# Another slot plan in an attention kernel: the 64-query tile third, V products in five slots, normalisation a slot later

## The chip, the cores and the metric

One core of a Trainium2 chip. The metric is the device time of one execution in microseconds (us). The whole computation is one program and one launch.

## The reference, cut to what matters

```python
def _attn_ref(q, k, v, w1, b1, w2):                      # q, k, v: (4, 8, 576, 64)
    scores = np.matmul(q, k.transpose(0, 1, 3, 2)) / np.sqrt(64)
    psi_rel = np.log1p(np.abs(pos[:, None] - pos[None, :]))
    psi_i = np.log1p(np.maximum(pos[:, None], 1.0))
    h = np.maximum((psi_rel / psi_i)[..., None] @ w1 + b1, 0.0)
    scores = scores + (h @ w2).transpose(2, 0, 1)[None]  # one bias table per head
    attn = np.exp(scores - np.max(scores, axis=-1, keepdims=True))
    attn = attn / (np.sum(attn, axis=-1, keepdims=True) + 1e-09)
    return np.matmul(attn, v)
x = attn_out.transpose(0, 2, 1, 3).reshape(2304, 512)
h = x @ w_in                                              # 512 -> 2048
out = (h * np.cos(h)) @ w_out                             # 2048 -> 512
```

## The kernel before

The program has three stages. The engines are named as in the profile: PE (TensorE), DVE (VectorE), ACT (ScalarE), POOL (GpSimd), SP (SyncE, which here only issues DMAs). Each engine runs its own instructions strictly in the order in which the program issues them.

**Bias (0 to about 61 us).** 36 groups of 16 query positions are computed and written to DRAM (`sc`), and read back as bias tiles by query tile: tile 4 (the last 64 queries) is computed first and loaded early (L348), tiles 0 to 3 are loaded in steps 19, 27, 35 and 36 of the loop (L346). The loop also turns the first keys and queries (`T_FIRST`, L335).

**Attention (about 61 to 346 us).** A *unit* is a pair of heads of one batch: 16 units (L71). A unit has five *slots* (L528), one for each tile of queries: tiles 0 to 3 have 128 queries for each of the two heads; tile 4 has the 64 last queries of both heads in one tile of 128 rows. `tiles` (L331) is the order of the tiles in the slots. `slot(i)` (L542) issues for every engine what belongs to slot `i` of 80 and works on several tiles at once:

- the tile of this slot (`now`): scores by `qk` (L380), in 12 matmuls (6 for tile 4), since queries and keys are split in a high and a low part (high x high, high x low of the keys, low of the queries x high, for each half of the columns and each head). DVE adds the bias and takes the minimum (L402; the scores are negated);
- the tile of the slot before (`last`): exponential and row sum on ACT (`softmax_exp`, L418); then the sum plus 1e-9 and its reciprocal on DVE (`recip`, L431), and the normalisation of the exponentials on POOL (`norm`, L439);
- the tile of three slots before (`prev`): transposes on PE (`ptrans`, L453; `ptrans_left`, L463), copied out of PSUM half by ACT and half by DVE (`keep_main`, L476; `keep_left`, L487);
- the product with V of an earlier unit (`pv`, L503), in five chunks of keys for each half of the queries; the fifth has the last 64 keys. `PV_EARLY` (L537) gives the chunks to slots: half 0 in slots 0 and 1, half 1 in slots 3 and 4, none in slot 2. ACT copies the result (`keep_x`, L523);
- the next units' queries and keys: the load (`LOAD_PLAN`, L538), the turn on PE (`T_EARLY`, L536; "x" is the last 64 positions of keys and queries), ACT's copy (`keep_turned`, L189), and the split in high and low parts on POOL (`split`, L163; `POOL_PLAN`, L529): step 0 gives the high part, steps 1 and 2 the low part of columns 0 to 319 and 320 to 639. Keys were turned two units ahead, queries one;
- one eighth of the first feed-forward weights in ten slots (`W_PLAN`, L539): these come as 64-bit floats and are converted by integer passes: `abs_w` on ACT (L89), steps 0, 0.5, 1 and 2 of `widen_w` on DVE (L99 to L105), step 3 on ACT (L107), step 4 on POOL (L109).

Scores have a ring of two PSUM buffers (`ps_s`, L365), one for each head. So a slot's product for head 0 can start when DVE has reduced head 0 of the slot before. Tile 4 uses one buffer; the other (`spare`, L414) takes the turned keys in that slot. Exponentials have four buffers (`pp`, L366).

**Feed-forward (about 346 us to the end).** 96 steps of two products on PE, with the cosine between them on ACT and DVE. Its first two steps (L774 to L779) are issued between the last slots of the attention; in unit 15 POOL already splits the feed-forward's input (`split_x`, L493), four parts in slots 0 to 3.

Of the kernel before, what the change touches and what calls it, by code (L numbers as in the profile page):

```python
# [23 lines left out]
def f(ap):  # L24
    return ap.bitcast(F32)
# [3 lines left out]
def kernel(  # L29
# [42 lines left out]
    NU = len(units)  # L72
# [16 lines left out]
    def abs_w(fc, part):  # L89
        b = wk.tile([128, 512], F32, tag="wb", name="wb")  # L90
        nc.scalar.activation(out=b, in_=f(raw[fc, part][:, :, 1]), func=AF.Abs)
        wabs[fc, part] = b
# [18 lines left out]
    with tc.manual_schedule():  # L111
# [27 lines left out]
        def load(u, x):  # L139
            hp, b = units[u]  # L140
            src = {"q": q, "k": k, "v": v}[x]
            pair_ = src[b, 2 * hp : 2 * hp + 2]
            if x == "v":
                t = vN[u % 2]
                for h in range(2):
                    nc.sync.dma_start(
                        out=t[:, 4 * h : 4 * h + 4, :], in_=pair_[h, 0:512].rearrange("(c p) d -> p c d", p=128)
                    )
                for h in range(2):
                    nc.sync.dma_start(out=t[64 * h : 64 * h + 64, 8, :], in_=pair_[h, 512:576])  # L150
                return
            m = 5 if x == "k" else 4
            t = (lk if x == "k" else ld).tile([128, m, 2, D], F32, tag=x, name=f"n{x}")
            for h in range(2):
                nc.sync.dma_start(out=t[:, 0:4, h], in_=pair_[h, 0:512].rearrange("(p r) d -> p r d", r=4))  # L155
            if x == "k":
                for i, o in ((k, 0), (q, 64)):
                    nc.sync.dma_start(
                        out=t[o : o + 64, 4], in_=i[b, 2 * hp : 2 * hp + 2, 512:576].rearrange("h p d -> p h d")
                    )  # L160
            nat[u, x] = t

        def split(u, x, step=None):  # L163
            n = turned[x]
            if x == "k":
                if u not in kN:
                    kN[u] = tp.tile([128, 2, 640], F32R, tag="kN", name="kN")
                o = kN[u]
            else:
                o = qTs[u % 2]  # L170
            if step in (None, 0):
                nc.gpsimd.tensor_scalar(o[:, 0], n, 1.0, 1.0, ALU.mult, ALU.mult)
            for i in range(2):
                c = slice(320 * i, 320 * i + 320)
                if step in (None, 1 + i):
                    nc.gpsimd.tensor_tensor(o[:, 1, c], n[:, c], f(o[:, 0, c]), ALU.subtract)
# [78 lines left out]
        wparts = [(fc, p) for fc in range(WPRE) for p in range(2)]  # L255
# [72 lines left out]
            )  # L328
            nc.sync.dma_start(out=sc[t][gi, :, 0 : RB - 1], in_=rt[:, 0 : RB - 1])

        tiles = [0, 1, 2, 3, 4]  # L331
        for i in range(WPRE):
            W[i] = wpre[i]
        ACT_H = [k for k in range(36) if k % 4 != 3]
        T_FIRST = {11: (0, "k"), 12: (0, "x"), 13: (0, "q"), 15: (1, "k")}  # L335
        S_FIRST = {13: "k", 14: "q"}
        todo = [(t, gi) for t in (4, 0, 1, 2, 3) for gi in range(len(groups[t]))]
        held, hts = None, bias_hid(0)
        for n in range(len(todo) + 1):
            now = hts  # L340
            if n < len(todo):
                hts = bias_hid(n + 1) if n + 1 < len(todo) else None
                ps = bias_rows(n, now)
            if held:
                bias_store(*held)
            if n in (19, 27, 35, 36):  # L346
                load_bias(0, (19, 27, 35, 36).index(n))
            if n == 11:  # L348
                load_bias(0, 4)
            held = (n, ps)  # L350
            if n == 6:
                for x in "kq":
                    load(1, x)
            if n in T_FIRST:
                keep_turned(T_FIRST[n][1], turn(*T_FIRST[n], bank()))
            if n in S_FIRST:
                split(0, S_FIRST[n])
            if n == 20:
                load(2, "k")
        stage.close()  # L360

        ps_t = opened(tail, "ps_t", 1, "left", PSUM)
# [68 lines left out]
        def recip(u, j, step):  # L431
            n = 2 if tiles[j] < 4 else 1
            if step == 0:
                nc.vector.tensor_scalar(dn[u, j][:, 0:n], dn[u, j][:, 0:n], 1e-9, None, ALU.add)
            else:
                rc[u, j] = sv.tile([128, 2], F32, tag="rc", name="rc")
                nc.vector.reciprocal(rc[u, j][:, 0:n], dn[u, j][:, 0:n])  # L437

        def norm(u, j, h):  # L439
            p, r = P[u, j], rc[u, j][:, h : h + 1]  # L440
            if tiles[j] == 4:
                nc.gpsimd.tensor_scalar(p[:, 576:640], p[:, 512:576], r, 1.0, ALU.mult, ALU.mult)
            p = p[:, 576 * h : 576 * h + 576]
            nc.gpsimd.tensor_scalar(p, p, r, 1.0, ALU.mult, ALU.mult)  # L444

        def heads_of(x):
            return range(2 if tiles[x[1]] < 4 else 1)
# [75 lines left out]
        def keep_x(u, hf):  # L523
# [4 lines left out]
        jobs = [(u, j) for u in range(NU) for j in range(5)]  # L528
        POOL_PLAN = [  # L529
            ([], []),  # L530
            ([("k", 0)], [("k", 1)]),
            ([], [("k", 2)]),
            ([("q", 0)], [("q", 1)]),
            ([("q", 2)], []),
        ]
        T_EARLY = [(1, "x"), None, (1, "q"), None, (2, "k")]  # L536
        PV_EARLY = [[(-1, 0, (0, 1))], [(-1, 0, (2, 3, 4))], [], [(-1, 1, (0, 1))], [(-1, 1, (2, 3, 4))]]  # L537
        LOAD_PLAN = [[(2, "q")], [(3, "k")], [], [], [(1, "v")]]  # L538
        W_PLAN = [("abs", 2), (0, 3), (0.5, 4), (1, 5), (2, 6), ("load", 6), (3, 7), (4, 7)]  # L539
        get = lambda i: jobs[i] if 0 <= i < len(jobs) else None  # L540

        def slot(i):  # L542
            u, j = divmod(i, 5)
            now, last, prev = get(i), get(i - 1), get(i - 3)
            if now:
                spare = qk(u, j)
            if last:
                for h in heads_of(last):
                    softmax_exp(*last, h)
            if prev:  # L550
                if prev[1] in (0, 2):
                    alloc_half(prev[0], prev[1] // 2)
                pm = ptrans(*prev)
            left = prev and tiles[prev[1]] < 4
            tu, tx = T_EARLY[j] or (0, None)
            tx = tx if now and u + tu < NU else None
            t = bank() if left or tx in ("x", "q") else None
            if left:
                pl = t[:, 0:128]
                ptrans_left(*prev, pl)  # L560
            if tx:
                pt = turn(u + tu, tx, {"x": t and t[:, 128:256], "q": t, "k": spare}[tx])
            for du, hf, chunks in PV_EARLY[j]:
                if 0 <= u + du < NU:
                    pv(u + du, hf, chunks)
            if prev:
                keep_main(*prev, 0, pm[0])
            if tx:
                keep_turned(tx, pt)
            for du, hf, chunks in PV_EARLY[j]:  # L570
                if 0 <= u + du < NU and 4 in chunks:
                    keep_x(u + du, hf)
            if last:
                recip(*last, 0)
                recip(*last, 1)
            if prev:
                keep_main(*prev, 1, pm[1])
            if left:
                keep_left(*prev, pl)
            for x, step in POOL_PLAN[j][0]:  # L580
                if u + 1 < NU:
                    split(u + 1, x, step)
            if last:
                for h in heads_of(last):
                    norm(*last, h)
            for x, step in POOL_PLAN[j][1]:
                if u + 1 < NU:
                    split(u + 1, x, step)
            if now:
                for du, x in LOAD_PLAN[j]:  # L590
                    if u + du < NU:
                        load(u + du, x)
                hp, b = units[u]
                if b == B - 1 and hp + 1 < HP:
                    load_bias(hp + 1, tiles[j])
                if u == NU - 1 and j < KD:
                    split_x(0, 0, j)
                for step, at in W_PLAN:
                    w, r = divmod(i - 0 - at, 10)
                    if r == 0 and 0 <= w < len(wparts):  # L600
                        if step == "load":
                            if w + 2 < len(wparts):
                                load_w(*wparts[w + 2])
                        elif step == "abs":
                            abs_w(*wparts[w])
                        else:
                            widen_w(*wparts[w], step)
# [226 lines left out]
```

## Time and profile before

| | |
|---|---|
| median of 3 runs | 756.83 us (754.45 to 757.5) |
| profiled execution | 754.29 us, its span 752.5 us |
| PE busy in the span | 716.7 us (95%) |
| DVE, ACT, POOL busy | 596.7, 442.2, 404.0 us |
| mean granted clock of PE | 0.981 |
| stretch 0 to 61 us (bias) | PE busy 50.59, DVE 49.16, ACT 46.07, POOL 5.87 us |
| stretch 61 to 345.63 us (attention) | PE busy 265.76, DVE 222.44, ACT 203.72, POOL 213.28 of 284.63 us |
| stretch 345.63 to 752.5 us (feed-forward) | PE busy 400.38, DVE 325.07, ACT 192.46, POOL 184.84 of 406.87 us |

The span is the time from the first to the last instruction of one execution. An engine is busy while an instruction of it runs. Ends of matmuls are modelled: successive ones overlap in the records by up to a tenth of a microsecond, so lengths from one start to the next are the better ones. "PEclk" is the share of TensorE's full clock that was granted: 1.00 is 2.4 GHz, 0.50 is 1.2 GHz. "[0.46 <-DVE m L402]" behind an instruction means that its engine stood idle 0.46 us before it, until the instruction of line 402 on DVE that writes `m` was done.

### The profile page before, as it was taken

The numbers are of one execution on the slowest core, as the hardware profiler recorded it, in microseconds if no ns is written. First come the engines' busy times: TensorE is split into PE (matmuls) and PEld (weight loads), VectorE is DVE, ScalarE is ACT, GpSimd is POOL, SyncE is SP. The second block draws the span as 40 slices with busy tenths as digits, with TensorE's granted clock in tenths as the row PEclk, the third lists the DMA queues.
The fourth block names the chain that finished last, engine by engine and source line by source line (L and its number), as shares of the span: only waits on it lengthen the run. The fifth ranks groups of instructions, "written<-read, shape, count | busy, mean of one in ns | idle before, by whom it ended". The sixth has DMA issues, their size and how long they took to land.

```text
span 752.5 us, 15721 instructions
## 1 busy us (share of the span) xinstructions
PE 716.7 (95%) x5786; PEld 574.4 (76%) x5786; DVE 596.7 (79%) x1307; ACT 442.2 (59%) x948; POOL 404.0 (54%) x486
## 2 busy tenths in 40 slices
PE   6987899999999999988999999999999999999997
PEld 3764666666666666657998989898888989899995
DVE  8964878788787878964779788899898998976655
ACT  6966577777787777753555555444545454533332
POOL 0203687777878777784256546364463554564300
PEclk9988799999999999999999999999999999999999
DMA  7776425432652551100010101010101011001112
GB/s 223 243 253 198 96 49 148 126 96 61 184 120 49 128 154 33 46 29 1 28 57 29 57 28 57 29 57 28 57 29 57 28 43 42 1 29 57 43 42 85
DMA packets 83917, 58.64 MB, mean 78 GB/s; under 512 B 61824, under 2 KB 70144, under 8 KB 83840
## 3 DMA queue, kind: packets, MB, share of 16 engines
q1 hardware_dynamic: 83840, 57.63, 27.2%
q8 instruction: 46, 0.75, 0.4%
q14 instruction: 31, 0.25, 0.1%
HBM read 42.00 MB, written 15.61 MB: 77 GB/s over the span
## 4 chain that ended last, share of the span: by engine, by line
PE 83%; DVE 10%; issue 3%; DMA 2%; ACT 1%; SPq 1%; POOL 0%; DVEq 0%; POOLq 0%; ACTq 0%
PE ph L636 26%; PE po L691 25%; PE pv L513 10%; PE s L389 9%; DVE P L402 5%; PE pm L451 5%; PE pa L307 4%; PE pt L464 2%; DMA sc<-rt 1%; PE spare L186 1%; DVE PT L474 1%; DVE ht L291 1%; DVE gl L665 1%; DMA nk<-in_k_dram 1%; SPq L155 1%
## 5 line engine op out<-in xcount | busy, mean ns | idle before, releaser
L402 DVE CUSTOM_DVE_ANT_0 P<-s,bt 128x576 f32<-128x576 f32 x144 | 103.9, 753 | 52.1 <-PE s L389 31.6
L444 POOL TENSOR_SCALAR P<-P,rc 128x576 f32<-128x576 f32 x144 | 112.5, 794 | 39.4 <-DVE rc L437 31.8
L640 ACT ACTIVATE a<-ph,quarter 128x384 int32<-128x384 f32 x96 | 55.8, 581 | 107.9 <-PE ph L636 106.7
L646 DVE SCALAR_TENSOR_TENSOR r<-a,ph 128x384 f32<-128x384 int32 x96 | 52.9, 551 | 77.7 <-ACT a L640 77.6
L422 ACT ACTIVATE P<-P,m 128x576 f32<-128x576 f32 x144 | 110.3, 770 | 5.7 <-DVE m L402 5.4
L498 POOL TENSOR_TENSOR xs<-xT,xs 128x384 fp32r<-128x384 f32 x96 | 107.0, 1114 | 8.0
L636 PE MATMUL ph<-xs,wpre 128*128 128x384 f32 x576 | 109.5, 338 | 0.9 <-DVE a L655 0.9
L389 PEld LDWEIGHTS s<-kN,qT 64*128 64x128 f32 (+1 forms) x864 | 71.9, 190 | 49.8 <-DVE m L402 24.6
L389 PE MATMUL s<-kN,qT 64*128 64x288 f32 (+1 forms) x864 | 95.4, 317 | 14.4 <-DVE m L402 13.5
L636 PE MATMUL ph<-xs,w 128*128 128x384 f32 x576 | 108.3, 337 | 0.5 <-DVE a L655 0.5
L636 PEld LDWEIGHTS ph<-xs,wpre 128*128 128x128 f32 x576 | 101.8, 188 | 7.1 <-DVE a L655 2.1
L636 PEld LDWEIGHTS ph<-xs,w 128*128 128x128 f32 x576 | 101.3, 188 | 5.6 <-DVE a L655 1.6
L651 ACT ACTIVATE r<-r,hpi 128x384 f32<-128x384 f32 x96 | 59.3, 618 | 69.7 <-DVE r L647 69.7
L497 POOL TENSOR_SCALAR xs<-xT 128x384 fp32r<-128x384 f32 x96 | 62.1, 646 | 45.9 <-PE ph L636 45.9
L513 PE MATMUL pv<-PT,vN 128*64 128x320 f32 (+1 forms) x512 | 77.3, 424 | 2.3 <-ACT PT L471 2.3
L691 PE MATMUL po<-w,gh 128*128 128x512 f32 x288 | 75.3, 396 | 0.0
L691 PE MATMUL po<-wpre,gh 128*128 128x512 f32 x288 | 75.2, 396 | 0.0
L665 DVE TENSOR_TENSOR gl<-a,gh 128x384 fp32r<-128x384 f32 x96 | 74.1, 772 | 0.6 <-ACT gh L659 0.6
L109 POOL TENSOR_TENSOR w<-wb,w 128x512 fp32r<-128x512 f32 x16 | 20.8, 1299 | 90.2 <-ACT w L107 90.2
L647 DVE SCALAR_TENSOR_TENSOR r<-a,r 128x384 f32<-128x384 int32 x96 | 61.8, 644 | 3.3
L659 ACT ACTIVATE gh<-a 128x384 fp32r<-128x384 f32 x96 | 49.9, 520 | 23.1 <-DVE a L655 22.3
L691 PEld LDWEIGHTS po<-w,gh 128*128 128x128 f32 x288 | 53.5, 188 | 8.9 <-ACT gh L659 0.2
(83 smaller groups left out, 1207.4 us busy)
## 6 DMA issues: line engine op xcount, KB each, us to landing
sc<-rt SPq DMA_DIRECT2D x36, 295.5 KB
raw<-in_moe_w_in_dram SPq DMA_DIRECT2D x16, 512.0 KB
raw<-in_moe_w_out_dram SPq DMA_DIRECT2D x16, 512.0 KB
bt<-sc SPq DMA_DIRECT2D x16, 288.0 KB
nk<-in_k_dram SPq DMA_DIRECT2D x32, 128.0 KB
nq<-in_q_dram SPq DMA_DIRECT2D x32, 128.0 KB
vN<-in_v_dram SPq DMA_DIRECT2D x32, 128.0 KB
bt<-sc SPq DMA_DIRECT2D x16, 256.0 KB
```

Source lines behind the costliest of these rows:

```text
L389: nc.tensor.matmul(s[h][:, hf, 0:HALF], qTs[u % 2][r, a, 128 * t : 128 * t + 128] if t < 4 else qTs[u % 2][:, a, 512:640], kN[u][r, b, o : ...
L402: nc.vector.tensor_tensor_reduce(neg.rearrange("p (a x) -> p a x", a=2), s[h][:, :, 0:HALF], bias[hp, t, h].rearrange("p (a x) -> p a x", ...
L422: nc.scalar.activation(out=P[u, j][:, 576 * h : 576 * h + 576], in_=neg, func=AF.Exp, bias=m[:, 0:1], scale=-1.0, accum_out=dn[u, j][:, h ...
L444: nc.gpsimd.tensor_scalar(p, p, r, 1.0, ALU.mult, ALU.mult)
L497: nc.gpsimd.tensor_scalar(h, src, 1.0, 1.0, ALU.mult, ALU.mult)
L498: nc.gpsimd.tensor_tensor(l, src, f(h), ALU.subtract)
L513: nc.tensor.matmul(ps[64 * h : 64 * h + 64, 0 : WQ[hf]], a, m, start=(c == 0), stop=(c == 4), tile_position=(r.start, 64 * h), skip_group_ ...
L636: nc.tensor.matmul(ps, a, x, start=(i == 0), stop=(i == 3 * KD - 1))
L647: nc.vector.scalar_tensor_tensor(r, n, -TWO_PI_LO, r, ALU.mult, ALU.add)
L651: nc.scalar.activation(out=r, in_=r, func=AF.Sin, scale=SIN_SCALE, bias=hpi)
L665: nc.vector.tensor_tensor(gl, a, f(G[key][0]), ALU.subtract)
L691: nc.tensor.matmul(O[n][i], a[:, 128 * i : 128 * i + 128], w, start=(i0 == 0 and p == 0), stop=(i0 == GF - 1 and p == 2),)
```

## The change

The order of the tiles becomes 0, 1, 4, 2, 3, so the 64-query tile is third and the spare score buffer falls into slot 2. Keys are turned one unit ahead, in slot 2, queries in slot 0 and the last 64 positions in slot 1; one turn of keys in the bias stage is dropped. POOL's splits move: queries to slots 2 and 3, keys to slots 3 and 4. V chunks go to all five slots. The loads of queries and keys move by one and two slots. The weight passes on DVE move to slots 0 and 2 (of an even and an odd unit), the two last steps to slot 3 of the odd unit, and the first `abs_w` to the end of the bias stage. The sum and reciprocal (`recip`) are now those of the tile of two slots before (`late`) and come first in the slot, ahead of the reductions on DVE; the normalisation follows on POOL in that slot, ahead of all splits.

```diff
@@ -328,11 +328,11 @@
             )
             nc.sync.dma_start(out=sc[t][gi, :, 0 : RB - 1], in_=rt[:, 0 : RB - 1])
 
-        tiles = [0, 1, 2, 3, 4]
+        tiles = [0, 1, 4, 2, 3]
         for i in range(WPRE):
             W[i] = wpre[i]
         ACT_H = [k for k in range(36) if k % 4 != 3]
-        T_FIRST = {11: (0, "k"), 12: (0, "x"), 13: (0, "q"), 15: (1, "k")}
+        T_FIRST = {11: (0, "k"), 12: (0, "x"), 13: (0, "q")}
         S_FIRST = {13: "k", 14: "q"}
         todo = [(t, gi) for t in (4, 0, 1, 2, 3) for gi in range(len(groups[t]))]
         held, hts = None, bias_hid(0)
@@ -357,6 +357,8 @@
                 split(0, S_FIRST[n])
             if n == 20:
                 load(2, "k")
+            if n == len(todo):
+                abs_w(*wparts[0])
         stage.close()
 
         ps_t = opened(tail, "ps_t", 1, "left", PSUM)
@@ -528,20 +530,23 @@
         jobs = [(u, j) for u in range(NU) for j in range(5)]
         POOL_PLAN = [
             ([], []),
-            ([("k", 0)], [("k", 1)]),
-            ([], [("k", 2)]),
+            ([], []),
             ([("q", 0)], [("q", 1)]),
-            ([("q", 2)], []),
+            ([("q", 2), ("k", 0)], []),
+            ([("k", 1), ("k", 2)], []),
         ]
-        T_EARLY = [(1, "x"), None, (1, "q"), None, (2, "k")]
-        PV_EARLY = [[(-1, 0, (0, 1))], [(-1, 0, (2, 3, 4))], [], [(-1, 1, (0, 1))], [(-1, 1, (2, 3, 4))]]
-        LOAD_PLAN = [[(2, "q")], [(3, "k")], [], [], [(1, "v")]]
-        W_PLAN = [("abs", 2), (0, 3), (0.5, 4), (1, 5), (2, 6), ("load", 6), (3, 7), (4, 7)]
+        T_EARLY = [(1, "q"), (1, "x"), (1, "k"), None, None]
+        PV_EARLY = [[(-1, 0, (0, 1))], [(-1, 0, (2, 3))], [(-1, 0, (4,))], [(-1, 1, (0, 1, 2))], [(-1, 1, (3, 4))]]
+        LOAD_PLAN = [[], [(2, "q")], [], [(3, "k")], [(1, "v")]]
+        W_PLAN = [("abs", -1), (0, 0), (0.5, 2), (1, 5), (2, 7), ("load", 7), (3, 8), (4, 8)]
         get = lambda i: jobs[i] if 0 <= i < len(jobs) else None
 
         def slot(i):
             u, j = divmod(i, 5)
-            now, last, prev = get(i), get(i - 1), get(i - 3)
+            now, last, late, prev = get(i), get(i - 1), get(i - 2), get(i - 3)
+            if late:
+                recip(*late, 0)
+                recip(*late, 1)
             if now:
                 spare = qk(u, j)
             if last:
@@ -570,20 +575,14 @@
             for du, hf, chunks in PV_EARLY[j]:
                 if 0 <= u + du < NU and 4 in chunks:
                     keep_x(u + du, hf)
-            if last:
-                recip(*last, 0)
-                recip(*last, 1)
             if prev:
                 keep_main(*prev, 1, pm[1])
             if left:
                 keep_left(*prev, pl)
-            for x, step in POOL_PLAN[j][0]:
-                if u + 1 < NU:
-                    split(u + 1, x, step)
-            if last:
-                for h in heads_of(last):
-                    norm(*last, h)
-            for x, step in POOL_PLAN[j][1]:
+            if late:
+                for h in heads_of(late):
+                    norm(*late, h)
+            for x, step in POOL_PLAN[j][0] + POOL_PLAN[j][1]:
                 if u + 1 < NU:
                     split(u + 1, x, step)
             if now:
```

## Rows read from the trace of the kernel before

**Rows 1.** Stretches: busy time of each engine, then granted clock, DMA share, GB/s.

```profile
core 0: us, PE busy (x) PEld busy (x) DVE busy (x) ACT busy (x) POOL busy (x), PEclk, DMA share, GB/s
61.00:80.49 19.49, 12.71 (x97) 9.66 (x97) 9.79 (x30) 10.14 (x25) 8.79 (x12) 0.68 0.64 154
99.08:312.27 213.19, 205.96 (x2352) 140.36 (x2350) 175.80 (x520) 162.95 (x428) 166.83 (x216) 1.00 0.41 101
312.27:345.63 33.36, 29.06 (x282) 18.95 (x281) 21.57 (x59) 17.81 (x41) 23.73 (x31) 0.95 0.14 42
324.00:327.00 3.00, 3.00 (x12) 1.21 (x11) 1.78 (x8) 2.11 (x5) 2.92 (x4) 0.50 0.00 0
345.63:752.50 406.87, 400.38 (x1994) 358.81 (x1992) 325.07 (x527) 192.46 (x350) 184.84 (x200) 1.00 0.13 41
```

**Rows 2.** Waits of PE, units 2 to 14: total us, times, longest us.

```profile
PE s L389 <- DVE m L402: 6.8, 20, 0.5
```

**Rows 3.** Timeline of PE, units 9 and 10: start, length, idle before.

```profile
222.81 0.40 PE L389 MATMUL s<-kN,qT 64*128 64x288 f32 x1 [0.46 <-DVE m L402]
...
223.48 1.06 PE L389 MATMUL s<-kN,qT 64*128 64x288 f32 x11 [0.28 <-DVE m L402]
...
228.36 0.60 PE L186 MATMUL spare<-ident,nk 128*128 128x128 f32 x4
...
230.81 1.07 PE L389 MATMUL s<-kN,qT 64*128 64x288 f32 x12
...
231.71 0.66 PE L451 MATMUL pm<-ident,P 64*128 64x64 f32 x16
...
232.67 1.08 PE L513 MATMUL pv<-PT,vN 128*64 128x256 f32 x8
...
233.68 1.06 PE L389 MATMUL s<-kN,qT 64*128 64x288 f32 x12
```

**Rows 4.** Timeline of ACT, unit 9: copy of the turned keys.

```profile
229.08 0.60 ACT L201 ACTIVATE kt<-spare 128x512 f32<-128x512 f32 x1 [0.18 <-PE spare L186]
```

**Rows 5.** Timeline of DVE, units 9 and 10.

```profile
217.76 1.19 DVE L103 SCALAR_TENSOR_TENSOR wb<-raw,wb 128x512 uint32<-128x512 uint32 x1
...
232.02 0.76 DVE L402 CUSTOM_DVE_ANT_0 P<-s,bt 128x576 f32<-128x576 f32 x1 [2.08 <-PE s L389]
...
233.38 0.15 DVE L434 TENSOR_SCALAR dn<-dn 128x1 f32<-128x1 f32 x1
...
233.64 0.67 DVE L474 COPY PT<-pm 128x512 f32<-128x512 f32 x1
...
234.23 0.28 DVE L474 COPY PX<-pt 128x128 f32<-128x128 f32 x1
```

**Rows 6.** Timeline of POOL, units 9 and 10.

```profile
220.78 1.91 POOL L444 TENSOR_SCALAR P<-P,rc 128x576 f32<-128x576 f32 x2 [1.24 <-DVE rc L437]
...
226.21 1.29 POOL L109 TENSOR_TENSOR wpre<-wb,wpre 128x512 fp32r<-128x512 f32 x1
...
227.48 0.73 POOL L172 TENSOR_SCALAR qT<-qt 128x640 fp32r<-128x640 f32 x1
...
228.18 1.47 POOL L444 TENSOR_SCALAR P<-P,rc 128x576 f32<-128x576 f32 x2
...
229.61 1.69 POOL L176 TENSOR_TENSOR qT<-qt,qT 128x320 fp32r<-128x320 f32 x2
...
233.92 0.32 POOL L442 TENSOR_SCALAR P<-P,rc 128x64 f32<-128x64 f32 x1 [1.17 <-DVE rc L437]
...
234.34 0.75 POOL L444 TENSOR_SCALAR P<-P,rc 128x576 f32<-128x576 f32 x1
```

**Rows 7.** Timeline of DVE, start of the attention.

```profile
73.54 0.76 DVE L402 CUSTOM_DVE_ANT_0 P<-s,bt 128x576 f32<-128x576 f32 x1 [4.49 <-DMA bt<-sc]
...
76.50 0.76 DVE L402 CUSTOM_DVE_ANT_0 P<-s,bt 128x576 f32<-128x576 f32 x1 [2.19 <-DMA bt<-sc]
```

**Rows 8.** Timeline of PE, first products of unit 1.

```profile
80.49 0.61 PE L389 MATMUL s<-kN,qT 64*128 64x288 f32 x1
...
81.31 1.80 PE L389 MATMUL s<-kN,qT 64*128 64x288 f32 x11 [0.21 <-ACT kt L201]
```

**Rows 9.** Timeline of PE, between attention and feed-forward.

```profile
342.64 2.37 PE L513 MATMUL pv<-PT,vN 128*64 128x320 f32 x16 [2.31 <-ACT PT L471]
```
## The prediction

> **What bounds the kernel now.** I read the stretches first [rows 1]. The feed-forward part (345.63 to 752.5 us) has TensorE (PE) busy 400.38 of 406.87 us at full clock, and the change touches nothing in it. Units 2 to 14 of the attention (99.08 to 312.27, cut at the first score product of units 2 and 15) take 213.19 us, 16.4 each. There PE is busy 97%, GpSimd (POOL) 78%, VectorE (DVE) 82%, so only what PE waits for can be won. All of PE's waits there are for DVE, 6.8 us in 20 [rows 2]. The timeline shows their place: in slot 3 the product finds its score banks not yet reduced, since slot 2 gives PE no V work to cover DVE [rows 3]. The first matmul goes out alone after 0.46 us, and the other head's starts 0.67 us after it, where a pair costs about 0.1. Beside the waits that loses some 0.3 us more a unit. So **PE alone** would need (213.19 - 6.8)/13 - 0.3 = 15.55 us a unit: 11.0 us is the most these 13 units can give. Around them two stretches are loose: the start (61 to 80.49: PE busy 12.71 of 19.49 us, mean clock 0.68) and the change to the feed-forward (312.27 to 345.63: busy 29.06 of 33.36) [rows 1].
>
> **The slots after the change.** PE's work in a unit is the same, placed otherwise. Slot 0 becomes 0.90 (scores: 230.81 to 231.71) + 0.41 (ten of the sixteen transposes of 0.66) + 0.60 (query turn, four transposes like the key turn at 228.36) + 1.01 (V: 232.67 to 233.68) = 2.92 us [rows 3]. Every slot now carries V work, so a next product comes about 2.9 us or more after the last. DVE begins a reduction 1.21 us after the product (230.81 to 232.02), takes 1.36 for two heads (to 233.38), and 0.59 + 0.28 for the two copies [rows 3, 5]. Banks are free 2.6 us after the product, and **the old wait is gone**. The sum and reciprocal (0.26, from 233.38 to 233.64) come ahead of the reductions, where DVE mostly waits for PE anyway, and no longer behind them waiting for ScalarE's (ACT's) exponentials.
>
> **What is late next: POOL.** The key splits are now in slots 3 and 4, and the next unit's third score matmul needs both halves of the low part (head 0 reads columns 64 to 352, across the cut at 320). So everything that POOL has in slots 2, 3 and 4 must be done when the next unit begins. It begins with the normalisation in slot 2, which waits for the reciprocal behind slot 1's DVE work: 2.92 (slot 0) + 1.21 + 1.36 + 0.59 + 0.28 = 6.36 us after the unit's start. From the sum to the normalisation 0.54 pass (233.38 to 233.92 [rows 5, 6]), so POOL starts at 6.90. Then it has normalisation 1.47, query high 0.73, half of the query's low part 0.85, normalisation 1.47, the other half 0.85, key high 0.73, normalisation of the 64-query tile 0.42 + 0.75 = 1.17, both key halves 1.69 [rows 6]: 8.96 us, **15.86 us** in all. That is the length of an even unit. An odd unit has the weight subtraction of 1.29 in slot 3 besides: **17.15 us**, of which PE stands idle 1.6 at the next unit's start. Units 2 to 14 then take 7 x 15.86 + 6 x 17.15 = 213.9 us, **0.7 us more** than now: the old wait is paid back as a wait for POOL. Ends: 202.2 us if POOL is in time (-11.0); and if both two-head normalisations of each chain took the 1.91 us of the longest row [rows 6] instead of 1.47, 13 x 0.88 = 11.4 more (+12.1). I take the sum of the usual durations, the 1.91 being one row among those of 1.47.
>
> One sentence of the Trainium skill speaks against that middle value. A 128x576 normalisation pair takes 1.47 us in one row and 1.91 in another, and the weight pass of DVE at 217.76 takes 1.19 us [rows 5, 6]. The page "SBUF — State Buffer", section "Who interferes with whom", states that a DVE instruction with two SBUF inputs and a GpSimd instruction that reads SBUF share a read interface, and the second to issue blocks until the first ends. By it the weight pass put into slot 2 of an odd unit (two inputs) could hold up the chain by its 0.44 us each time, and the sum would be 6 x 0.44 = 2.6 us worse.
>
> **Weight passes** move from slots 3 and 4 (even) and 0 and 1 (odd) to slots 0 and 2. In slot 0, DVE is through 1.21 + 1.36 + about 0.6 for the smaller copies = 3.2 us after the start; a pass of up to 1.19 ends at 4.4, and the reciprocal (0.26) makes 4.65, where the next reduction could begin at 2.92 + 1.21 = 4.13. So the POOL start is put off by 0 to 0.5 us; I take 0, POOL having little in slots 0 and 1 to hold the pass up with. The end of it lies inside the range above.
>
> **Key turn.** Its bank is the other half of the score ring and must be copied before slot 3's second head. ACT ends the copy 1.32 us after the turn's start (228.36 to 229.68 [rows 3, 4]); in the new slot 2 PE has about 1.1 us of work there. That is 0.2 us a unit, hidden as long as POOL sets the unit's length, 2.6 us in all otherwise.
>
> **Loads.** The queries' load moves from slot 0 to 1 and is used in the next unit's slot 0 (13 us later instead of 19), the keys' from slot 1 to 3, and is used about 29 us later. Both stay ahead of the V load on the SP queue, whose wait for slot 4's V products is unchanged. Cost nothing; without the cover PE's turn would wait for the landing. The moved `abs_w` lies on ACT ahead of unit 0, where ACT is busy 10.14 of 19.49 us [rows 1]: nothing. The removed early key turn saves PE about 0.5 us in the bias stage, which ends on stores; I count nothing.
>
> **Start.** Today DVE stands 4.49 and 2.19 us for the bias of tile 3, whose second half is there at 76.50 [rows 7], with the 64-query tile still to do; unit 1's second matmul starts at 81.31 [rows 8]. With tile 3 last, the other tile is done inside that stall, and unit 1 can go on when the reduction ends, at 77.2: 4.1 us sooner. But PE is at half clock there (1.80 us instead of 1.06 [rows 3, 8]), and unit 1's busy slots now begin with it: I take 2.2 us lost (between 1.4, what unit 1 pays today, 99.08 - 81.31 - 16.4, and 2.9, all of slot 0). Then 77.2 + 17.15 + 2.2 = 96.6 against 99.08: **-2.5 us** (0 to -3.6).
>
> **End.** Today the stretch of 33.36 us has 4.3 us idle and 3.0 us at half clock (1.5 lost) [rows 1]: 5.8 us, of which 2.31 is the wait behind the first sine [rows 9]. After it, unit 15's splits of the feed-forward input (about 1.6 us a slot) still hold up a normalisation by 0.8 and the 64-query tile's by 1.2, and the sine's wait is covered by one V chunk and a full tile more (1.5 left): 3.5 us. Makes **-2.3 us** (0 to -5.8).
>
> **Sum:** -2.5 + 0.7 - 2.3 = -4.1 us. The profiled execution took 754.29 us (752.5 in the span, 1.8 around it), 2.5 less than the median of 756.83; taken from the median: 752.7. A measurement of this kernel can tell about 0.5%, 3.8 us, from no change.
>
> **Rivals.**
> *PE sets the pace.* POOL is in time, units take 15.55 plus the 0.2 of the key copy: 202.2 + 2.6 - 213.2 = -8.4; with start and end -13.2, **743.6 us**. For it: PE's loop is what the old plan was near. Against: 8.96 us of POOL after 6.90 don't fit into 15.55. Chance 0.12.
> *POOL slower than its usual rows.* One long normalisation a chain (0.44) and 0.2 of the put-off start: 13 x 0.64 = 8.3 us more, **761 us** at the worst, some 757 with half of it: no change. For it: weight passes of DVE now lie in slot 2 beside it, and 1.91 was seen. Against: even units have 0.3 us between PE's loop and the chain only. Chance 0.22.
> *The clock falls in the new wait.* PE's stand of 1.6 us at the start of units 2, 4, ..., 14 is followed by half clock, as between 324 and 327 us today, after some 2 us of broken idle: 3 us at half clock, 1.5 lost [rows 1]. Seven times 10.5 us: -4.1 + 10.5 = +6.4, **763 us, slower**. It decides from the point where a stand grows to some 2 us with other gaps near it. Against: 2.31 us in one piece with dense work on both sides left the matmuls after it at full clock (16 in 2.37 us [rows 9]). The Trainium skill, "TensorE: Matmul & The Clock Gate", "A second HAM failure mode: psum-queue depth-cycling", tells of kernels whose small stands between groups make the clock swing; the row of 324 agrees, that of 342 does not. Chance 0.16.
>
> **The numbers.** My forecast (749 to 756) has 0.50; 0.35 of it lies over 0.5% below the median, 0.15 within. Faster: 0.35 + 0.12 = 0.47. Same: 0.15 + 0.20 of the slow-POOL case = 0.35. Slower: 0.16 + 0.02 = 0.18. The range of 745 to 761 leaves out half of the first rival and most of the third.
>
> **What would show it.** Right: no PE wait for DVE's minimum in slot 3; PE waiting at the first products of a unit for POOL's key split (L176), about 0.3 us into even units' successors and 1.6 after odd ones; units alternating near 15.9 and 17.2; the bias wait of DVE in one slot later, and unit 1 near 77 us; feed-forward's third step some 4 us earlier. Wrong: units of 15.6 us, a granted clock below 1 inside units 2 to 14, or the wait for DVE still there.

## The result and the profile after

The changed kernel took **761.91 us** (median of 12 runs, 758.22 to 767.14) against 756.46 us for the kernel before in the same session (12 runs, 754.45 to 757.86): 1.0073 times as long, 95% interval 1.0054 to 1.0092. It is slower by 0.7%. The forecast was 752.7 and the range ended at 761. In a later set of ten executions of the changed kernel one ran at a mean granted clock of 0.753 and took 860.14 us; it is left out of every comparison.

The execution that was profiled took 760.39 us, its span 758.3, which is 5.8 us more than the span of before. The page's busy times, and the first lines of its chain of work that ended last:

```profile
PE 713.8 (94%) x5786; PEld 573.3 (76%) x5786; DVE 598.9 (79%) x1307; ACT 445.5 (59%) x948; POOL 397.6 (52%) x486
...
PE 71%; POOL 11%; DVE 7%; DMA 5%; issue 3%; ACT 1%; SPq 1%; DVEq 0%; POOLq 0%; ACTq 0%
PE ph L635 26%; PE po L690 25%; PE s L391 7%; PE pv L515 5%; POOL P L446 5%; DMA sc<-rt 3%; PE pm L453 3%; POOL kN L176 3%; PE pa L307 3%; POOL qT L176 2%; PE pt L186 1%; POOL wpre L109 1%; DVE wb L101 1%; PE pt L466 1%; DVE P L404 1%
```

Each engine runs as many instructions as before, and busy times moved by few us: PE 2.9 and POOL 6.4 less than before, DVE 2.2 and ACT 3.3 more. But POOL is now 11% of the chain: normalisations (L446), splits of keys and queries (L176) and the weight subtraction (L109). In the kernel before it had no part in it:

```profile
PE 83%; DVE 10%; issue 3%; DMA 2%; ACT 1%; SPq 1%; POOL 0%; DVEq 0%; POOLq 0%; ACTq 0%
```

The lines of the helpers named here are two higher than before (L389 is now L391).

Where the 5.8 us are is seen from stretches with the bounds of [rows 1]: the first product of unit 2, that of unit 15, the third feed-forward step, the end. In the changed kernel a unit's first two matmuls go out early and the third waits, so a unit's start is taken here, and below, as the start of its third matmul less some 0.15 us for these two. After the length come the busy times of PE, PEld, DVE, ACT and POOL, then the granted clock, the DMA share and GB/s.

```profile
99.10:319.95 220.85, 207.09 (x2353) 142.77 (x2353) 179.94 (x519) 164.98 (x427) 161.13 (x215) 0.99 0.40 97
...
319.95:351.56 31.61, 27.27 (x279) 18.46 (x279) 20.80 (x59) 18.50 (x43) 23.67 (x32) 1.00 0.16 44
351.56:758.30 406.74, 400.37 (x1994) 358.87 (x1992) 324.67 (x527) 192.42 (x350) 184.78 (x200) 1.00 0.13 41
```

Units 2 to 14 take 220.85 us where they took 213.19: **+7.7**. The change to the feed-forward takes 31.61 instead of 33.36: -1.75. The feed-forward itself is the same to 0.13 us. The start comes out even: the first score product comes at 63.43 instead of 60.91 (+2.5), and from there to unit 2 it is 35.67 instead of 38.17 (-2.5). PE's timeline shows the first product, and the point at which unit 1's first product can go on. DVE's timeline shows the last wait for tile 3's bias, which ends at 78.78 instead of 76.50 [rows 7]:

```profile
63.43 1.05 PE L391 MATMUL s<-kN,qT 64*128 64x288 f32 x12 [0.55 <-ACT rt L322]
...
79.60 1.81 PE L391 MATMUL s<-kN,qT 64*128 64x288 f32 x11 [1.89 <-DVE m L404]
```

```profile
78.78 0.76 DVE L404 CUSTOM_DVE_ANT_0 P<-s,bt 128x576 f32<-128x576 f32 x1 [1.79 <-DMA bt<-sc]
```

All waits of PE in units 2 to 14 (total us, times, longest), and those of POOL for its normalisations there:

```profile
PE s L391 <- POOL kN L176: 15.3, 13, 2.0
```

```profile
POOL P L446 <- DVE rc L439: 29.3, 26, 2.5
POOL P L446 <- PE s L391: 14.4, 9, 2.6
POOL P L446 <- ACT P L424: 11.2, 4, 3.3
POOL P L446 <- PE pt L466: 2.5, 6, 0.4
```

POOL's four rows are one kind of wait: whatever the profile names there, each of the 45 ends 0.18 to 0.20 us after a reciprocal of DVE (L439). On PE the wait for DVE's minimum [rows 2] is gone, and a wait for POOL's key split stands in its place, more than twice as large. The timeline of PE shows its place (start, length, then the idle time before and what ended it):

```profile
206.58 1.06 PE L391 MATMUL s<-kN,qT 128*128 128x288 f32 x6
...
216.37 0.40 PE L391 MATMUL s<-kN,qT 64*128 64x288 f32 x2
217.03 0.94 PE L391 MATMUL s<-kN,qT 64*128 64x288 f32 x10 [0.27 <-POOL kN L176]
...
222.68 1.06 PE L391 MATMUL s<-kN,qT 128*128 128x288 f32 x6
225.59 1.30 PE L391 MATMUL s<-kN,qT 64*128 64x288 f32 x12
...
232.46 0.40 PE L391 MATMUL s<-kN,qT 64*128 64x288 f32 x2
234.83 0.93 PE L391 MATMUL s<-kN,qT 64*128 64x288 f32 x10 [1.97 <-POOL kN L176]
...
240.47 1.06 PE L391 MATMUL s<-kN,qT 128*128 128x288 f32 x6
```

The product of 128x288 is slot 2's. From one to the next is one length of a unit: 16.10 us with an even unit's POOL work between them (206.58 to 222.68), 17.79 with an odd one's (222.68 to 240.47). From unit 2's product to unit 14's all the lengths agree with these two to 0.02 us, but for one of 19.15 that is explained below. Two matmuls of a unit go out, the third waits for the low part of the keys: 0.27 us, then 1.97. In slot 3 (225.59) nothing waits for DVE any more.

The chain that PE waits for is on POOL. Here are parts of it in even unit 8 and odd unit 9:

```profile
207.61 1.47 POOL L446 TENSOR_SCALAR P<-P,rc 128x576 f32<-128x576 f32 x2 [1.19 <-DVE rc L439]
...
209.85 0.93 POOL L176 TENSOR_TENSOR qT<-qt,qT 128x320 fp32r<-128x320 f32 x1
211.20 1.47 POOL L446 TENSOR_SCALAR P<-P,rc 128x576 f32<-128x576 f32 x2 [0.42 <-DVE rc L439]
...
215.29 1.68 POOL L176 TENSOR_TENSOR kN<-kt,kN 128x320 fp32r<-128x320 f32 x2
...
223.88 1.47 POOL L446 TENSOR_SCALAR P<-P,rc 128x576 f32<-128x576 f32 x2 [1.09 <-PE s L391]
...
226.12 1.19 POOL L176 TENSOR_TENSOR qT<-qt,qT 128x320 fp32r<-128x320 f32 x1
227.73 1.46 POOL L446 TENSOR_SCALAR P<-P,rc 128x576 f32<-128x576 f32 x2 [0.42 <-PE pt L466]
229.16 0.88 POOL L176 TENSOR_TENSOR qT<-qt,qT 128x320 fp32r<-128x320 f32 x1
...
230.70 1.30 POOL L109 TENSOR_TENSOR wpre<-wb,wpre 128x512 fp32r<-128x512 f32 x1
...
233.09 1.68 POOL L176 TENSOR_TENSOR kN<-kt,kN 128x320 fp32r<-128x320 f32 x2
```

The chain is the one that was worked out, from slot 2's normalisation to the two key halves. But it is not in one piece. The first half of the queries' low part, split in slot 2, takes 1.19 us in the odd unit, where the second half takes 0.88. And in both units POOL stands idle 0.42 us ahead of slot 3's normalisation. What DVE does there:

```profile
209.97 0.83 DVE L436 TENSOR_SCALAR dn<-dn 128x2 f32<-128x2 f32 x1
...
220.16 0.69 DVE L103 SCALAR_TENSOR_TENSOR wb<-raw,wb 128x512 uint32<-128x512 uint32 x1
220.77 0.16 DVE L436 TENSOR_SCALAR dn<-dn 128x2 f32<-128x2 f32 x1
...
225.36 1.22 DVE L105 SCALAR_TENSOR_TENSOR wb<-raw,wb 128x512 uint32<-128x512 uint32 x1
226.50 0.83 DVE L436 TENSOR_SCALAR dn<-dn 128x2 f32<-128x2 f32 x1
227.37 0.17 DVE L439 RECIPROCAL rc<-dn 128x2 f32<-128x2 f32 x1
```

Beside an idle POOL (220.16) a weight pass takes 0.69 and the sum behind it 0.16. In slot 2, beside POOL's splits, a pass of the same shape takes 1.22 and the sum 0.83. So the reciprocal that slot 3's normalisation needs ends at 227.54, 0.23 us after POOL is through with the split (227.31). At the lengths of 220.16 it would have ended some 0.98 us after the start of the pass, at 226.34, and POOL would not have stood.

### The profile page after: what moved, and what is told of

Its sections match the earlier page's. It is cut to its first block, busy times and chain, and to the rows that moved or that the text cites. A ratio compares the mean times of both kernels' runs of the same rounds, so it can differ in the third digit from the quotient of the medians.

```text
span 758.3 us, 15679 instructions
## 1 busy us (share of the span) xinstructions
PE 713.8 (94%) x5786; PEld 573.3 (76%) x5786; DVE 598.9 (79%) x1307; ACT 445.5 (59%) x948; POOL 397.6 (52%) x486
## 4 chain that ended last, share of the span: by engine, by line
PE 71%; POOL 11%; DVE 7%; DMA 5%; issue 3%; ACT 1%; SPq 1%; DVEq 0%; POOLq 0%; ACTq 0%
PE ph L635 26%; PE po L690 25%; PE s L391 7%; PE pv L515 5%; POOL P L446 5%; DMA sc<-rt 3%; PE pm L453 3%; POOL kN L176 3%; PE pa L307 3%; POOL qT L176 2%; PE pt L186 1%; POOL wpre L109 1%; DVE wb L101 1%; PE pt L466 1%; DVE P L404 1%
## 5 line engine op out<-in xcount | busy, mean ns | idle before, releaser
L446 POOL TENSOR_SCALAR P<-P,rc 128x576 f32<-128x576 f32 x144 | 106.5, 751 | 105.1 <-ACT P L424 48.9
L391 PEld LDWEIGHTS s<-kN,qT 64*128 64x128 f32 (+1 forms) x864 | 71.5, 188 | 60.1 <-POOL kN L176 21.5
L391 PE MATMUL s<-kN,qT 64*128 64x288 f32 (+1 forms) x864 | 95.5, 319 | 22.4 <-POOL kN L176 15.5
L664 DVE TENSOR_TENSOR gl<-a,gh 128x384 fp32r<-128x384 f32 x96 | 74.9, 780 | 0.6 <-ACT gh L658 0.6
L473 ACT ACTIVATE PT<-pm 128x512 f32<-128x512 f32 (+1 forms) x80 | 44.3, 554 | 45.3 <-PE pm L453 45.3
L109 POOL TENSOR_TENSOR w<-wb,w 128x512 fp32r<-128x512 f32 x16 | 20.7, 1295 | 89.9 <-ACT w L107 89.9
```

What stands on the lines that cost most here:

```text
L391: nc.tensor.matmul(s[h][:, hf, 0:HALF], qTs[u % 2][r, a, 128 * t : 128 * t + 128] if t < 4 else qTs[u % 2][:, a, 512:640], kN[u][r, b, o : ...
L664: nc.vector.tensor_tensor(gl, a, f(G[key][0]), ALU.subtract)
```

## The experiments

The theory on record from the first runs on is that units 2 to 14 are as long as POOL's chain from slot 2's normalisation to the key split, lengthened by the weight passes in slot 2. The rivals are that the wait itself makes PE's clock fall, and that the late normalisation or the plan costs by itself. Lengths of units are from one product of the 64-query tile to the next, the one with an even unit's chain first. Each ratio is to the kernel before in the same session.

**Half of the queries' split out of the chain.** The last query half goes behind the key halves.

```diff
-            ([("q", 2), ("k", 0)], []),
-            ([("k", 1), ("k", 2)], []),
+            ([("k", 0)], []),
+            ([("k", 1), ("k", 2), ("q", 2)], []),
```

> POOL theory (the normalisations and splits that POOL has in slots 2, 3 and 4 end with the key split and set the unit's length; measured 16.1 us for even units, 17.8 for odd): the second half of the queries' low part, 0.84 us, now follows the key split, so the chain is 0.84 shorter. Odd units 16.95, even units down to PE's own pace of about 15.65; units 2 to 14 take 211.3 instead of 220.9 us, the execution about 753 to 754. The wait of PE for L176 after odd units falls from 2.0 to about 1.1 us and is gone after even ones. Rival (the wait for POOL only shows that the units are slow for another reason, for instance DVE with the sum and reciprocal ahead of its reductions): the wait moves to another releaser and the time stays within 2 us of 761.

Measured: 751.84 us, 0.9943 of the kernel before (0.9921 to 0.9964); units 15.62 and 16.96. PE's waits in units 2 to 14:

```profile
PE s L391 <- POOL kN L176: 6.7, 6, 1.1
```

A split of 0.88 less in the chain made odd units 0.82 shorter, and even ones 0.48, nearly to the length of PE's own work (15.55). So the chain sets the pace of the changed kernel.

**The weight subtraction out of the chain**, into the next unit's slot 0.

```diff
-        W_PLAN = [("abs", -1), (0, 0), (0.5, 2), (1, 5), (2, 7), ("load", 7), (3, 8), (4, 8)]
+        W_PLAN = [("abs", -1), (0, 0), (0.5, 2), (1, 5), (2, 7), ("load", 7), (3, 8), (4, 10)]
...
+                if i == len(jobs) - 1:
+                    widen_w(*wparts[-1], 4)
```

> POOL theory: the weight subtraction (1.27 us, in slot 3 of odd units) goes to slot 0 of the next unit, where POOL mostly waits. Odd units 17.8 - 1.27 = 16.5, even units unchanged at 16.1 or 0.1 longer: units 2 to 14 take about 212 us, the execution about 754. PE's wait after odd units is 0.7 us or less. Rival (something else): no change within 2 us.

Measured: 749.29 us, 0.9913 (0.9887 to 0.9939); units 16.13 and 16.55. The odd unit is 1.24 us shorter, nearly the subtraction's 1.30; the even one, which has no subtraction, is not shorter.

**Both edits of the last two together.**

> POOL theory: both moves together, chain 2.1 us shorter in odd units and 0.84 in even ones; every unit then runs at PE's pace of about 15.65 to 15.8 us, units 2 to 14 take 204 to 206 us, the execution 745 to 748: below both kernels. PE's wait for L176 is under 2 us in all. Rival: within 2 us of 761. If DVE's order sets the pace instead, units stop at some 16 us with a wait for DVE.

Measured: 742.62 us, 0.9842 (0.9798 to 0.9887); units 15.73 and 16.01; PE waits for the key split 1.2 us in all.

**No weight pass in slot 2.** The two passes are left out, so part of the weights is not converted.

```diff
-        W_PLAN = [("abs", -1), (0, 0), (0.5, 2), (1, 5), (2, 7), ("load", 7), (3, 8), (4, 8)]
+        W_PLAN = [("abs", -1), (0, 0), (1, 5), ("load", 7), (3, 8), (4, 8)]
```

> Leaves out the two weight passes of DVE that the plan has in slot 2 (the shift-and-mask of even units and the sign pass of odd ones), so the first four weight blocks are not converted fully. Theory of the mutual hold-up (POOL's query split and DVE's weight pass and sum delay one another in slot 2, so that the normalisation of slot 3 starts late): the split takes 0.87 again instead of 0.93 and 1.19, the sum 0.17 instead of 0.83, POOL's gap of 0.42 ahead of slot 3's normalisation is gone; even units 15.8, odd units 17.1, units 2 to 14 about 213 us, the execution about 755. Rival (DVE's passes are hidden, the chain is long by its own work alone): no more than 1 us is won.

Measured: 751.23 us, 0.9932 (0.9909 to 0.9956); units 15.64 and 17.04. The same place of the odd chain on POOL:

```profile
222.74 0.88 POOL L176 TENSOR_TENSOR qT<-qt,qT 128x320 fp32r<-128x320 f32 x1
223.60 1.47 POOL L446 TENSOR_SCALAR P<-P,rc 128x576 f32<-128x576 f32 x2
```

The split is back at 0.88, and the normalisation follows at once. The passes beside POOL thus cost 0.46 us in an even unit and 0.74 in an odd one: 7 x 0.46 + 6 x 0.74 = 7.7 us in units 2 to 14. Without them these units would be 1.5 us shorter than in the kernel before (7 x 15.64 + 6 x 17.04 = 211.7 against 213.19). The run takes out the pass and its hold-up together; that it is the hold-up rests on the lengths above.

**Each half of the change alone.** First the late sum, reciprocal and normalisation on the old plan (the kernel before with these lines of `slot`):

```diff
+            if late:
+                recip(*late, 0)
+                recip(*late, 1)
...
-            if last:
-                recip(*last, 0)
-                recip(*last, 1)
...
-            for x, step in POOL_PLAN[j][0]:
-                if u + 1 < NU:
-                    split(u + 1, x, step)
-            if last:
-                for h in heads_of(last):
-                    norm(*last, h)
-            for x, step in POOL_PLAN[j][1]:
+            if late:
+                for h in heads_of(late):
+                    norm(*late, h)
+            for x, step in POOL_PLAN[j][0] + POOL_PLAN[j][1]:
```

> The kernel before with only the second half of the change (sum, reciprocal and normalisation a slot later and first; splits behind it). POOL theory: in the old plan the keys are split in slots 1 and 2 and the low part of the first query columns in slot 3, long before the next unit needs them, so POOL does not set the pace; the old wait for DVE in slot 3, which comes from the missing V work in slot 2, stays. Units of about 16.2 and 16.6 as before, the execution 753 to 757, same as before. Rival (the late normalisation itself is the harm): slower than before by 4 us or more.

Measured: 757.03 us, 1.002 (0.9997 to 1.0043), no difference; units 16.13 and 16.73. The old wait stays:

```profile
PE s L389 <- DVE m L402: 8.1, 20, 0.7
```

Then the new plan with these lines as before (the changed kernel with the lines above undone):

> The changed kernel with the sum, reciprocal and normalisation where they were (the tile of one slot before, behind the reductions; the first list of splits ahead of the normalisation). POOL theory: the key split of slot 4 then does not stand behind a normalisation of that slot; the key split ends about 14.9 us after an even unit's start and 16.1 after an odd one's (12.0 for the reciprocal of the 64-query tile, 1.17, the subtraction 1.27 in odd units, 1.69). Even units at PE's pace of 15.7 to 15.9, odd ones 16.2 to 16.4: units 2 to 14 about 209 us, the execution 747 to 750, faster than before. Rival (the slot plan itself is slow): 758 or more.

Measured: 748.59 us, **0.9911** (0.9884 to 0.9937); units 15.55 and 16.70. The start of POOL's chain in an odd unit that begins at 212.04:

```profile
218.40 1.47 POOL L446 TENSOR_SCALAR P<-P,rc 128x576 f32<-128x576 f32 x2 [1.34 <-DVE rc L439]
...
220.54 1.89 POOL L446 TENSOR_SCALAR P<-P,rc 128x576 f32<-128x576 f32 x2
```

The chain starts 6.4 us into the unit (7.0 in the changed kernel: 223.88 less the unit's start, 217.03 - 0.15 = 216.88), and the next normalisation finds its reciprocal ready. That normalisation is itself held up (1.89 instead of 1.47), yet the unit is 1.1 us shorter. So the plan alone gives 0.9%; the later normalisation, which costs nothing by itself, turns that into a loss of 0.7%.

**Splits ahead of the late normalisation.** If the order on POOL is what costs, the splits need not wait behind a normalisation that waits for DVE.

```diff
+            for x, step in POOL_PLAN[j][0]:
+                if u + 1 < NU:
+                    split(u + 1, x, step)
             if late:
                 for h in heads_of(late):
                     norm(*late, h)
-            for x, step in POOL_PLAN[j][0] + POOL_PLAN[j][1]:
+            for x, step in POOL_PLAN[j][1]:
```

> The changed kernel with one thing moved: the first list of splits is issued to POOL ahead of the slot's normalisation, as in the kernel before. POOL theory: the splits of slots 2 and 3 need not wait for the reciprocal, and the key split of slot 4 no longer stands behind the 64-query tile's normalisation (1.17): even units at PE's pace of about 15.65, odd ones 15.7 to 16.0; units 2 to 14 about 205 us, the execution 744 to 747. Rival (the hold-up between DVE and POOL in slot 2 is the main thing): odd units 17 or more, the execution above 752.

Measured: 743.19 us, 0.9841 (0.9813 to 0.9869); units 15.55 and 15.94. PE no longer waits for the key split in units 2 to 14. On POOL the key halves now stand ahead of the 64-query tile's normalisation:

```profile
220.74 1.70 POOL L176 TENSOR_TENSOR kN<-kt,kN 128x320 fp32r<-128x320 f32 x2
222.40 0.33 POOL L444 TENSOR_SCALAR P<-P,rc 128x64 f32<-128x64 f32 x1
```

**The same with the weight subtraction in the next unit** (this edit and the second one).

> As the run before, with the weight subtraction in slot 0 of the next unit as well. POOL theory: all units at PE's pace of about 15.65, no wait for L176, execution 742 to 745: no more than 2 us better than one of the two moves alone with the other (742.6 us was measured for the query half last and the subtraction moved). If PE's pace is not the floor, it goes below 740.

Measured: **739.28 us, 0.9786** (0.9758 to 0.9815), the fastest of all. PE's waits in units 2 to 14, and two of its units:

```profile
PE s L391 <- DVE m L404: 1.1, 1, 1.1
```

```profile
213.15 1.06 PE L391 MATMUL s<-kN,qT 128*128 128x288 f32 x6
...
228.71 1.06 PE L391 MATMUL s<-kN,qT 128*128 128x288 f32 x6
```

Every unit takes 15.55 to 15.57 us, the length that was worked out for PE alone, but one of 17.02, where DVE waited 0.90 us for a bias tile (144.33).

**The changed kernel once more, and with the early key turn put back.** The second is to tell whether the removed turn made the first product late.

```diff
-        T_FIRST = {11: (0, "k"), 12: (0, "x"), 13: (0, "q")}
+        T_FIRST = {11: (0, "k"), 12: (0, "x"), 13: (0, "q"), 15: (1, "k")}
```

> The changed kernel once more, unaltered, for a second profile. Jitter theory of the start: the first score product (63.43 us in the first profile, 60.91 in the kernel before) comes anywhere between 61 and 64 us, since six other profiles with the same bias stage have it at 61.0 to 63.7. Clock rival: besides the one fall seen (a unit of 19.15 instead of 17.78 us), this profile has other falls at other units after the waits of 2 us; if every wait brought one, six units would be 1.4 us longer. I expect none to two. Units 16.1 and 17.8, the execution 758 to 765.

> The changed kernel with the key turn of unit 1 issued in the bias stage again (in addition: slot 2 of unit 0 turns the same keys once more). Jitter theory: the first product comes between 61 and 64 us and the time is within 2 us of the changed kernel's. Rival (the dropped turn, which cost PE and ACT about 0.5 us each, shifted the bias stage's stores so that it ends 1.5 to 2.5 us later): first product near 61 us and the execution 1.5 us or more below the changed kernel's.

Measured: the changed kernel took 762.87 us (nine executions), 1.0076 (1.0052 to 1.0099). No trace of these nine is kept, so the two questions put to this run stay unanswered. With the turn the time is 762.39 us, 1.0083 (1.0056 to 1.011), and the first product comes at 62.75. The turn wins nothing, so it is not the cause. Over the other profiles the first product came at 60.91 and 61.32 with the old bias stage, and at 61.03 to 63.67 in nine with the new one, with or without the turn. Whether the change makes it later on average stays open.

The profile with the turn put back says something about the clock. The wait at the start of a unit is the same each time, but not what follows. First two units of the changed kernel, then one of this run:

```profile
133.16 0.93 PE L391 MATMUL s<-kN,qT 64*128 64x288 f32 x10 [1.96 <-POOL kN L176]
...
302.60 1.57 PE L391 MATMUL s<-kN,qT 64*128 64x288 f32 x10 [1.95 <-POOL kN L176]
```

```profile
132.92 1.57 PE L391 MATMUL s<-kN,qT 64*128 64x288 f32 x10 [1.94 <-POOL kN L176]
```

Ten matmuls take 0.93 us, or 1.57 when PE goes on at its lower level (granted clock 0.50 from 302.60 to 305.00). That happened after one of seven waits of 1.8 to 2.0 us in the changed kernel (its unit took 19.15 us instead of 17.78, +1.4) and after two of seven in this run (132.92 and 303.64). In the profiles with waits of up to 1.2 us at that place no matmul of these products was slow.

## Why the prediction was wrong

**The step that failed** is the term "units 2 to 14 ... 0.7 us more" in "What is late next: POOL": it measured 7.7. The mechanism was right: the old wait went, POOL's key split took its place at the third score matmul, and units alternate. The chain was mis-sized. Predicted were 15.86 and 17.15 us a unit, measured 16.1 and 17.8: 7 x 0.25 + 6 x 0.63 = 5.5 us, and one fall of the clock 1.4, makes 6.9 above the 0.7. Between the two profiled executions the forecast was -4.1 and the result +5.8. Of these 9.9 us 6.9 are this term, 2.5 the first product, which came later, and 0.5 the end.

- *Start of the chain*: 6.90 us after the unit's start predicted; 7.0 measured in the odd unit (223.88 - 216.88), 6.8 in the even one (207.61 - 200.78). Right.
- *Length of the chain*: 8.96 and 10.25 us predicted, 9.36 (207.61 to 216.97) and 10.89 (223.88 to 234.77) measured. The durations were taken from rows in which POOL worked undisturbed, and as one piece. Measured are 0.42 us in which POOL stands idle in each unit, and in the odd one a split of 1.19 instead of 0.85. Without the slot-2 passes units take 15.64 and 17.04, 0.1 to 0.2 under the sum: the durations were good, the neighbour was left out.
- *The long normalisation*: "the 1.91 being one row among those of 1.47" misreads the kernel before. Of the 52 two-head normalisations of its units 2 to 14, 33 took 1.5 us, 13 took 1.6 to 1.7 and six 1.9, one in each odd unit, each with a weight pass (L105) beside it. So the hold-up came in every odd unit before the change too, and its price could be read there. Beside the one at 220.78 [rows 6] DVE has:

```profile
221.29 0.78 DVE L105 SCALAR_TENSOR_TENSOR wb<-raw,wb 128x512 uint32<-128x512 uint32 x1
```

- *Weight passes*: "I take 0, POOL having little in slots 0 and 1 to hold the pass up with". For the pass in slot 0 this is what the row at 220.16 shows (0.69). The pass in slot 2 was left at no cost in the sum, though the prediction itself named it. What DVE's pass delays is not only POOL's split but also the sum and reciprocal queued behind it on DVE, for which POOL's next normalisation waits. That second way was not seen; it is 0.42 us in every unit, more than the first (some 0.3 in odd units, 0.05 in even ones).
- The Trainium skill, "SBUF — State Buffer", "Who interferes with whom", was quoted against the middle value with 2.6 us for the odd units. The trace agrees for the pass, which has two inputs: 1.22 us beside POOL's splits, 0.69 beside an idle POOL. By the same section of the Trainium skill a tensor_scalar can take the shared ports too. The sum is one, with a single input, and its 0.83 against 0.16 us agrees; this is most of what holds up the even unit.
- *Start*: -2.5 was predicted, and counted from the first product it is -2.5: unit 1 goes on 16.2 us behind it (16.3 predicted), and unit 2 starts 19.5 us after that (19.4 predicted). But the first product itself came 2.5 us later in this profile, so none of it is left.
- *End*: -2.3 predicted, -1.75 measured. The wait for the 64-query tile's normalisation is 1.34 us (1.2 predicted), another normalisation's 0.35 (0.8 predicted), but the one ahead of the last V products, 2.31 in the kernel before [rows 9], is 2.51 where 1.5 was expected. It ends now with DVE's copy, and ahead of that copy L664 took 1.34 us where it took 0.55 in the kernel before (L665 there, 341.59):

```profile
336.52 0.53 PE L453 MATMUL pm<-ident,P 64*128 64x64 f32 x10 [1.34 <-POOL P L446]
...
348.57 2.38 PE L515 MATMUL pv<-PT,vN 128*64 128x320 f32 x16 [2.51 <-DVE PT L476]
```

```profile
346.48 1.34 DVE L664 TENSOR_TENSOR gl<-a,gh 128x384 fp32r<-128x384 f32 x1
```

- *Key turn, loads*: slot 3's product takes 1.30 us instead of 1.06, the 0.2 us that was predicted, hidden here behind POOL. No wait for a load appears.

**The rivals.** "POOL slower than its usual rows" is what came, by the neighbour that it named. Its price of 0.64 us for each unit, 8.3 in all, covers the 5.5 that the chains were too long; the time passed its 761 us only with the late first product, the fall of the clock and the end. That its 0.64 is also the odd unit's excess is luck: it was made of a longer normalisation and a later start, and the two-head normalisations of units 2 to 14 all took some 1.47 us. It had a chance of 0.22, since the usual rows were believed. "The clock falls in the new wait" happened, in one and two of seven waits, not in all: some 1.4 us each, not the 10.5 in all that would have made it the cause. The Trainium skill's "TensorE: Matmul & The Clock Gate", "A second HAM failure mode: psum-queue depth-cycling", tells of small stands between groups of matmuls that make the clock swing; the traces agree for three of these fourteen waits. "PE sets the pace" did not come with this change. The version of 739.28 us reaches it, with units of 15.55 us where this rival had 15.75: slot 3's product takes 1.30 us there too, so PE alone is some 0.2 us shorter than was worked out.

## What to carry to other kernels

When a wait of the busiest engine is removed, work out the next chain with its queue order, and see what stands in front of the item that is due: here splits that were due stood behind normalisations that waited for another engine, and putting them first turned +0.7% into -1.6%. A duration of GpSimd or VectorE holds only for the neighbour that it was measured beside; if a change moves two such instructions side by side, price the hold-up for both, and for what is queued behind each. Before a long row is set aside as an exception, count how often it comes and look at what runs beside it: one long row in every second unit is a price. Two edits that are worth -0.9% and nothing alone can be worth +0.7% together, so try each half.

## What the runs showed that was not expected

- A sum on 128x2 elements that takes 0.16 us took 0.83 beside a split on POOL, in both units shown (209.97, 226.50). A tiny instruction was held up longer (by 0.67 us) than the large pass ahead of it (1.22 instead of 0.69).
- PE's wait of 1.8 to 2.0 us at a unit's start is followed by full clock eleven times and by half clock three times in two executions. In the ten runs with the early turn, the two longest (767.44 and 767.32 us) have the lowest mean clocks, 0.975 and 0.972. The mean clock alone does not order the times: one execution of the changed kernel took 762.54 us at 0.931.
